# Matmuls on a constant tile in the front of a linear-attention kernel, and a new order of its loads and steps

## The chip, the cores and the metric

One Trainium2 chip, of which the program uses one core. A core has five engines that run side by side: TensorE (PE, with its weight loads as PEld), VectorE (DVE), ScalarE (ACT), GpSimd (POOL) and SyncE (SP), and 16 DMA engines that all queues share. The metric is the device time of one execution in microseconds. The kernel before took a median of 246.48 us in three runs (246.47 to 247.59).

## What is computed

Linear attention with an elu feature map over 8 batches, 8 heads, 576 positions and 64 channels, and then a multiplicative feed-forward layer on its 4608 x 512 output:

```python
def phi(x):
    return np.where(x > 0, x, np.exp(x) - 1.0) + 1.0
q_p, k_p = (phi(q), phi(k))
kv = np.einsum('bhsd,bhse->bhde', k_p, v)
z = np.sum(k_p, axis=2)
num = np.einsum('bhsd,bhde->bhse', q_p, kv)
den = np.einsum('bhsd,bhd->bhs', q_p, z)[..., None] + 1e-06
x = num / den                      # then heads side by side: 4608 x 512
a = x @ w1                         # 512 x 1024
b = x @ w2                         # 512 x 1024
h = a * b @ w3                     # 1024 x 1024
out = h @ w_out                    # 1024 x 512
```

Inputs and output are float32; the products run in bfloat16.

## The kernel before

**The work.** w3 and w_out are first multiplied into one matrix wf of 1024 x 512, so that each token goes through w1 and w2, a product of the two, and wf. The 8 batches are 8 chunks of 512 tokens; what is left of each batch (64 tokens) makes a ninth chunk. The core works through attention of batch b, then the feed-forward units of its chunk, with several chunks under way at a time.

**The order is written out by hand.** `ORDER` (from L585) is a string of steps. `step` (L638) issues each in turn, so the string gives the order on every engine and on every queue; each engine runs its own instructions strictly in that order. A step is a letter, a number, often a second number after a dot, and sometimes a `+`, which chooses another engine or queue. The letters that the text uses:

- `E i`: load row tile i of w3 (`load_w3`, L135), on POOL's queue. `w i`: eight transposes of it on PE and a copy (`w3_tr`, L145). `C x`: load a quarter of w_out (`load_wo`, L130), on POOL's queue. `u i.p`: two of the eight matmuls of row tile i of wf (`wf_mm`, L152); the copy out of PSUM comes behind the last pair.
- `L`, `M`, `N` with b.g: load half g of k, q or v of batch b (`load_qkv`, L99). With `+`, and for v of the first two batches always, the load goes on POOL's queue, else on SP's. `R b.0` is the tail of q and k as four DMAs of 64 KB, `R b.1` the tail of v as two (`load_tail`, L110); with `+` on POOL's queue. The text calls them tail pieces.
- `B x.p`: load the quarter x of the columns of w1 (p = 0) or w2 (p = 1), on POOL's queue (`load_w12`, L124).
- `X`/`x`, `Y`/`y`, `Z`/`z` with b.g: exponential (ACT), max (DVE) and min (DVE) of phi, for q (capital) and k; g = 2 is the tail, for both. `v b.g`: a copy of v, with g = 2 the tail.
- `a b.g`: transposes of phi(q) on PE and a copy. `T b.0`: the same by DMA, for later batches. `K b`: kv of a batch (`kv_full`, L228) on PE and two copies. `A b.j`: numerator and denominator of a block (`nat`, L289) on PE (tile nd) and the division on DVE; j = 4 is the tail. `P b.j`: transposes of the result on PE (tile xtp) and a copy. `D`: the same by DMA.
- `F c.f`: a unit of the feed-forward layer, four matmuls with w1 and four with w2 of 512 columns (`f_unit`, L380), then a copy on ACT and a product on DVE. F c.f reads the column quarter x = f/2, rounded down, of w1 and w2: F0.7 and F0.6 read B3, F0.5 and F0.4 B2, F0.3 and F0.2 B1. `h0` to `h3` are units 0 and 1 of chunk 0, four matmuls a step, and read B0; `i` closes them.
- `G`, `m`, `d`, `e`: the units of chunks 3 to 8 in a form with fewer products, and what prepares them. `O c.m`: eight matmuls with wf; `S`, `H`, `Q`: stores of the output. `I`: constants.

**Constants.** `I1` writes vrs[0], a tile of 128 x 520, with zeros and ones (four memsets; L88 and L90). `v0.2` later writes the tail of batch 0's v into parts of it.

**Buffers.** PSUM holds four banks that wf, F and some nd tiles share (`mm_ps`), one pair (`at_ps`) for kv and nd, and two banks, "o" and "u", for transposes and O units. Each tile waits until its bank's earlier reader is through.

**Two gates.** `GATES` makes SP's load M2.1 wait until B0.0 has landed, and R6.0 until the transposes T3.0. A gated load holds back what is behind it on SP.

**Order of the loads before.** On POOL: E4 E3 C0 E1 E0 C1 C2 C3 E5 E6 L0.1 E2 E7 M0.1 L0.0 N0.1 N0.0 M1.1 M1.0 R1.0 B3.0 L1.0 B3.1 N1.1 L1.1 R1.1 N1.0 B2.0 B2.1 B1.0 B0.0 B1.1 B0.1 R2.0 R3.0. On SP, at the same time: M0.0 R0.1 R0.0, and from M2.1 on the loads of the later batches.

Of the kernel before, what the change touches and what calls it, by code (L numbers as in the profile page):

```python
# [20 lines left out]
def kernel(  # L21
# [56 lines left out]
    def constants(part, alt):  # L78
# [6 lines left out]
        else:  # L85
# [3 lines left out]
            for g in range(2):  # L89
                eng.memset(vrs[part - 1][g * R:(g + 1) * R, :, g, :, D:E1], 1.0)  # L90
# [505 lines left out]
    y3.2 z3.2 N3.1 v2.1 F1.2 O0.1+ N3.0 S0.0 e0.2 K2 F1.5 A2.2 Z3.1 x3.0 F1.4 A2.1+ F1.1 x3.1 A2.0+
    y3.0 O0.3 T3.0 S0.1 y3.1 A2.3+ D2.0 z3.0 z3.1 v3.2 v3.0 v3.1 O1.2+ O1.3 R4.1 e1.3 R6.0+ M4.0
    M4.1 e0.0 e0.1 e0.3 K3 O1.0 A3.1+ O1.1 L4.0 A3.2+ e1.2 F2.1 A3.0+ N4.1 F2.5 A3.3+ D3.0 Y4.0 L4.1
    v4.2 F2.7 S1.1 N4.0 Y4.1 y4.2 X4.1 Z4.1 F2.2 A2.4+ x4.2 X4.0 F2.0 v4.1 z4.2 Z4.0 T4.0 F2.3 M5.1
    d3.2 L5.0 M5.0 S1.0 y6.2 L5.1 d3.0 R5.0+ F2.4 y5.2 d3.1 x6.2 x4.0 y4.0 z4.0 G3.1.1 F2.6 A3.4+  # L600
    v4.0+ y4.1 G3.1.3 x4.1 z4.1 G3.1.2 x5.2 O2.2 G3.1.4 z5.2 d3.3 G3.1.5 m3.1.5 G3.0.4 G3.0.1 K4
    z6.2 G3.0.3 G3.1.6 G3.1.7 A4.2+ G3.0.5 N5.0 y5.0 R5.1+ v5.2 m3.0.5 G3.0.2 Y5.1 X5.1 O2.3 S2.1
    G3.0.7 x5.0 Z5.1 G3.0.6 z5.0 Y5.0 A4.0+ X5.0 Z5.0 O2.1 m3.0.6 x5.1 O2.0 y5.1 L6.0 N5.1 L6.1
    G3.3.1 G3.3.4 S2.0 T5.0 A4.1+ z5.1 G3.2.1 m3.1.6 G3.3.3 G3.2.4 G3.2.3 G3.3.5 G3.3.2 v5.0 G3.2.5
    A4.3+ D4.0 G3.3.7 G3.2.2 v5.1 G3.3.6 G3.2.7 G3.2.6 m3.2.5 m3.2.6 x6.1 O3.1 x6.0 K5 m3.3.5 M6.1
    D1.1 m3.3.6 O3.3 y6.0 z6.0 y6.1 A5.2 z6.1 O3.2 d4.0 d4.1 d4.2 A5.0+ d4.3 G4.1.1 G4.1.4 R6.1 X6.1
    Y6.1 Z6.1 D3.1 O3.0 A5.1+ G4.1.3 G4.1.6 G4.0.1 G4.1.5 v6.2 G4.0.4 A5.3 G4.0.3 G4.1.7 G4.0.2
    G4.0.5 N6.0 v6.0 m4.1.5 G4.1.2 G4.3.1 G4.0.6 G4.0.7 A4.4+ G4.3.3 N7.1 G4.3.4 M6.0 Y6.0 G4.2.1
    G4.3.5 D5.0 d5.0 G4.3.6 X6.0 Z6.0 N6.1 G4.2.3 G4.2.2 G4.2.4 S3.1 G4.3.7 G4.2.5 v6.1 G5.0.4 d5.1
    m4.1.6 G4.2.6 G5.1.1 G4.2.7 m4.3.6 d5.2 K6 m4.3.5 L7.0 m4.0.5 G5.0.1 m4.2.5 G5.1.2 L7.1 d5.3  # L610
    G5.1.3 m4.0.6 G5.0.3 G5.0.6 G5.1.4 G5.0.5 G5.0.2 G5.1.5 G5.0.7 m4.2.6 G4.3.2 T6.0 A6.3+ G5.1.7
    y7.1 S3.0 x7.0 x7.1 O4.2 A6.0 R7.0 O4.1 y7.0 G5.2.1 z7.0 A6.2 z7.1 G5.1.6 G5.3.1 N7.0 G5.3.4
    G5.2.3 A6.1 G5.3.3 G5.2.2 G5.2.4 G5.3.5 x7.2 G5.2.5 G5.3.2 M7.1 G5.3.7 X7.1 M7.0 G5.2.6 m5.0.6
    G5.2.7 Y7.0 m5.2.5 R7.1 v7.2 m5.1.6 m5.1.5 m5.3.5 D6.0 d6.2 d6.0 Y7.1 A5.4+ O4.3 S4.1 d6.1
    m5.2.6 v7.1 O4.0 y7.2 z7.2 Z7.1 X7.0 Z7.0 G6.1.1 v7.0 G6.1.4 G5.3.6 O5.0 G6.1.3 G6.3.4 T7.0 S4.0
    m5.0.5 G6.1.6 d6.3 G6.0.1 D5.1 G6.1.2 A6.4+ m5.3.6 G6.1.5 G6.0.3 G6.0.4 G6.2.4 G6.0.5 K7+ G6.1.7
    G6.0.7 m6.1.6 G6.0.2 A7.1 G6.3.1 O5.2 G6.3.3 G6.0.6 G6.2.1 G6.3.5 G6.3.2 A7.4 G6.2.3 G6.3.7
    m6.0.6 G6.2.2 G6.2.6 G6.2.5 m6.2.5 O5.1 D7.1 m6.1.5 d8.0 G6.3.6 G6.2.7 d8.1 m6.3.6 S5.0 A7.3+
    O5.3 G8.0.1 G8.0.4 G8.1.1 d8.2 A7.0 G8.0.3 G8.0.6 G8.1.3 d8.3 G8.0.5 G8.1.4 G8.1.5 S5.1 G8.2.4
    G8.0.7 G8.0.2 G8.1.7 G8.1.2 m6.2.6 G8.2.1 G8.1.6 m6.0.5 G8.3.1 m6.3.5 G8.2.3 G8.2.6 G8.3.3  # L620
    m8.1.5 G8.2.5 G8.3.4 G8.3.5 G8.3.2 G8.2.7 A7.2+ G8.2.2 G8.3.7 D7.0 d7.0 m8.0.6 O6.2 O6.1 O6.0
    S6.0 O6.3 G7.0.1 d7.1 d7.3 d7.2 G8.3.6 m8.3.6 G7.1.1 S6.1 G7.0.3 G7.0.4 m8.3.5 G7.1.3 G7.0.5
    m7.0.5 G7.1.4 G7.1.5 G7.0.6 G7.0.7 G7.0.2 G7.1.7 G7.1.6 G7.2.1 G7.1.2 m8.0.5 G7.3.1 m8.1.6
    G7.2.3 G7.2.4 G7.3.3 m8.2.6 G7.3.4 G7.2.5 G7.2.2 G7.3.2 G7.3.5 G7.2.7 G7.3.6 G7.2.6 G7.3.7 O7.0
# [7 lines left out]
    def loaded(s, ins):  # L632
        s = s.rstrip("+")
        if s in gates:
            after(ins, held[gates[s]])
        held[s] = ins

    def step(s):  # L638
        alt = len(s) - len(s.rstrip("+"))
# [4 lines left out]
        if t == "F":
            f_unit(b, i)
        elif t == "G":
            g_unit(b, i, int(at[1]))
        elif t == "m":
            g_mul(b, i, int(at[1]), alt)
        elif t == "e":  # L650
            ws_make(b, i, alt)
        elif t == "d":
            xs_make(b, i, alt)
        elif t == "O":
            o_unit(b, i, alt)
        elif t == "V":
            w_unit(b, i)
        elif t == "s":
            s_make(b, i, alt)
        elif t == "S":  # L660
            o_store(b, i)
        elif t == "H":
            o_store(b, i // 2, i % 2)
        elif t == "Q":
            o_last(b, i)
        elif t == "I":
            constants(b, alt)
        elif t == "w":
            w3_tr(b, alt)
        elif t == "u":  # L670
            wf_mm(b, i, alt)
        elif t == "t":
            wt_make(b)
        elif t in "LMN":
            name = "kqv"["LMN".index(t)]
            loaded(s, load_qkv(name, b, i, alt))
        elif t == "R":
            loaded(s, load_tail(b, i, alt))
        elif t == "B":
            loaded(s, load_w12(b, i))  # L680
        elif t == "C":
            loaded(s, load_wo(b))
        elif t == "E":
            loaded(s, load_w3(b))
        elif t in "xX":
            phi_exp("kq"["xX".index(t)], b, i)
        elif t in "yY":
            phi_max1("kq"["yY".index(t)], b, i, alt)
        elif t in "zZ":
            phi_min("kq"["zZ".index(t)], b, i)  # L690
        elif t == "v":
            v_unit(b, i, alt)
        elif t == "T":
            held[s] = qt_load(b, i)
        elif t == "a":
            q_tr(b, i, alt)
        elif t == "K":
            kv_full(b, alt)
        elif t == "A":
            nat(b, i, alt)  # L700
        elif t == "D":
            xt_load(b, i)
        elif t == "P":
            xt_tr(b, i, alt)
        elif t == "h":
            if b == 0:
                held["h"] = [f_open(0, 0), f_open(0, 1)]
            for f in range(2):
                for ps, w in zip(held["h"][f], (w1_sb, w2_sb)):
                    f_mm(0, f, ps, w, b)  # L710
        elif t == "i":
            f_close(0, b, *held["h"][b])

    nc.scalar.preload_act_table_set("natural_log_exp_and_others")
    for s in ORDER.split():
        step(s)
# [28 lines left out]
```

## Time and profile before

| what | value |
|---|---|
| median of three runs | 246.48 us |
| the profiled execution | 246.08 us |
| its span, first to last instruction | 244.3 us |
| PE busy | 227.1 us (93%), 1675 matmuls |
| DVE busy | 190.0 us (78%) |
| ACT busy | 159.1 us (65%) |
| POOL busy | 37.5 us (15%) |
| mean granted TensorE clock | 0.992 |
| DMA moved | 49.46 MB, 202 GB/s in the mean |

Times inside the trace count from the first instruction, so a step at 47 us is 47 us into the span. In a row of a timeline stand the start, the duration from first start to last end, the engine, the line, the operation, the tiles it writes and reads, the shape, and the count; in brackets the idle time of the engine ahead of it, and what ended that. Matmuls overlap in the pipeline, so a price per matmul is taken from start to start, not from durations. A row of waits has who waited at which line, for whom, the total in us, how often, and the longest. A row of busy time by stretch has the stretch, its length, then busy time and count of PE, PEld, DVE, ACT and POOL, the granted clock, the DMA share (the sum over packets under way, so it can be over 1) and GB/s.

### The profile page before, as it was taken

The page shows a single profiled execution, that of the slowest core. Times are in us where ns is not written, and L with a number is a line of the kernel's source. Part 1 is how long each engine was busy: PE and PEld are TensorE (multiplying, and loading weights), DVE is VectorE, ACT ScalarE, POOL GpSimd, SP SyncE. Part 2 cuts the span into 40 slices and gives each one's busy share as a digit, 9 for nine tenths or more (in the row PEclk, how much of TensorE's full clock was granted, in tenths as well). Part 3 has the DMA queues.
Part 4 walks back from the last instruction along what each step waited for, and adds up shares of the span by engine and source line. Part 5 has one row for each costly group of instructions (what it writes and reads, how often), then busy time and mean ns, then how long its engine had stood idle before and what let it go on. Part 6 is the DMA issues. An engine that isn't in the chain of part 4 may idle for free.

```text
span 244.3 us, 4627 instructions
## 1 busy us (share of the span) xinstructions
PE 227.1 (93%) x1675; PEld 146.8 (60%) x1692; DVE 190.0 (78%) x416; ACT 159.1 (65%) x296; POOL 37.5 (15%) x61
## 2 busy tenths in 40 slices
...
GB/s 159 192 201 301 296 234 240 196 241 309 287 197 290 263 196 275 214 289 270 370 366 192 243 244 292 237 248 157 86 198 10 107 90 0 89 172 0 3 196 149
DMA packets 68343, 49.46 MB, mean 202 GB/s; under 512 B 37088, under 2 KB 63456, under 8 KB 68320
## 3 DMA queue, kind: packets, MB, share of 16 engines
...
## 4 chain that ended last, share of the span: by engine, by line
PE 67%; DMA 15%; DVE 7%; ACT 6%; issue 2%; POOL 1%; SPq 0%; DVEq 0%; ACTq 0%; POOLq 0%
PE o_ps L544 21%; PE gu L429 14%; PE gt L429 10%; PE a_ps L366 7%; PE b_ps L366 7%; DMA k<-in_k_dram 5%; DMA q<-in_q_dram 5%; PE nd L311 3%; DMA wt_sb<-in_moe_w_out_dram 3%; DMA v<-in_v_dram 3%; ACT e L181 2%; PE kvp L246 1%; DVE spare L464 1%; ACT spare L461 1%; DVE y L186 1%
## 5 line engine op out<-in xcount | busy, mean ns | idle before, releaser
L544 PE MATMUL o_ps<-wf_sb,ab 128*128 128x512 bf16 x266 | 63.1, 379 | 0.8
L544 PEld LDWEIGHTS <-ab 128*128 128x128 bf16 x280 | 26.9, 98 | 29.1 <-DVE ab L468 0.8
L546 ACT COPY o_sb<-o_ps 128x512 f32<-128x512 f32 x31 | 18.1, 585 | 26.1 <-PE o_ps L544 24.9
L429 PEld LDWEIGHTS <-w_sb 128*128 128x128 bf16 x288 | 27.9, 98 | 5.7 <-issue 0.9
L366 PEld LDWEIGHTS <-w_sb 128*128 128x128 bf16 x192 | 18.4, 100 | 20.2 <-issue 1.7
L366 PE MATMUL a_ps<-xt,w_sb 128*128 128x512 bf16 x96 | 26.5, 389 | 0.0
L366 PE MATMUL b_ps<-xt,w_sb 128*128 128x512 bf16 x96 | 26.1, 384 | 0.0
L330 DVE TENSOR_TENSOR xn<-nd,r 128x512 bf16<-128x512 f32 x30 | 20.7, 691 | 2.1
L372 DVE TENSOR_TENSOR ab<-a_sb,b_ps 128x512 bf16<-128x512 f32 x24 | 16.2, 684 | 6.5 <-PE b_ps L366 3.3
L429 PEld LDWEIGHTS <-wt_sb 128*128 128x128 bf16 x192 | 18.2, 98 | 4.0 <-issue 0.2
L429 PEld LDWEIGHTS <-spare 128*128 128x128 bf16 x192 | 18.7, 98 | 2.2
L181 ACT ACTIVATE e<-q 128x1024 bf16<-128x1024 f32 x16 | 16.9, 1059 | 3.7 <-DMA q<-in_q_dram 3.7
L473 DVE TENSOR_TENSOR ab<-spare 128x256 bf16<-128x256 f32 x48 | 18.5, 418 | 0.1
L429 PE MATMUL gu<-spare,wt_sb 128*128 128x256 bf16 x96 | 18.3, 272 | 0.1
L429 PE MATMUL gu<-spare 128*128 128x256 bf16 x96 | 18.3, 272 | 0.0
L311 PE MATMUL nd<-kv,qt 128*128 128x130 bf16 (+1 forms) x160 | 15.9, 221 | 2.5 <-DVE r L317 1.2
L371 ACT COPY a_sb<-a_ps 128x512 f32<-128x512 f32 x24 | 13.7, 584 | 6.5 <-PE a_ps L366 6.4
L464 DVE TENSOR_TENSOR spare<-spare,gu 128x512 f32<-128x512 f32 x24 | 16.2, 680 | 2.0 <-PE gu L429 1.9
L464 DVE TENSOR_TENSOR spare<-spare,gt 128x512 f32<-128x512 f32 x24 | 16.2, 680 | 1.9 <-PE gt L429 1.9
L181 ACT ACTIVATE e<-k 128x1024 bf16<-128x1024 f32 x16 | 16.9, 1060 | 0.4 <-DMA k<-in_k_dram 0.3
L156 PE MATMUL wf_ps<-wt_sb,w3t 128*128 128x512 bf16 x61 | 16.2, 408 | 0.9 <-DMA wt_sb<-in_moe_w_out_dram 0.7
L311 PEld LDWEIGHTS <-qt 128*128 128x128 bf16 (+1 forms) x160 | 11.0, 99 | 9.7 <-DVE xn L330 4.7
...
## 6 DMA issues: line engine op xcount, KB each, us to landing
...
```

Source lines behind the costliest of these rows:

```text
L156: nc.tensor.matmul(wfs[i], w3ts[i][:, kc, :], wo_sb[:, kc, :], start=(kc == 0), stop=(kc == FC - 1))
L181: nc.scalar.activation(out=e, in_=x, func=AF.Exp)
L311: nc.tensor.matmul(nds[g][rows, i * 2 * E1:(i + 1) * 2 * E1], w, kvs[b % 2][:, i, g].rearrange("p u e -> p (u e)"), start=True, stop=True)
L330: nc.vector.tensor_tensor(out=dst.rearrange("p (g h) e -> p g h e", g=2), in0=v4[:, :, :, 0:D], in1=r[rows].unsqueeze(3).to_broadcast([n, ...
L366: nc.tensor.matmul(ps, w[:, kc, f * P:(f + 1) * P], xt_of(c)[:, :, kc, :], start=(kc == 0), stop=(kc == KC - 1))
L371: nc.scalar.copy(out=a_sb, in_=a_ps)
L372: nc.vector.tensor_mul(out=abs_[c][:, f, :], in0=a_sb, in1=b_ps)
L429: nc.tensor.matmul(t[:, w], l, r, start=(first and w == 0 and k == 0), stop=(k == 1), skip_group_check=True)
L464: nc.vector.tensor_tensor(out=s, in0=s, in1=t, op=ALU.add)
L473: (nc.gpsimd if alt else nc.vector).tensor_mul(out=abs_[c][:, f, r * HN:(r + 1) * HN], in0=s[:, 0], in1=s[:, 1])
L544: nc.tensor.matmul(o_ps, ab[:, f, m * P:(m + 1) * P], wf_sb[:, f, :], start=(f == 0), stop=(f == FC - 1))
L546: copy_of(alt)(out=rows_of(c, m // 2)[:, m % 2], in_=o_ps)
```

## The change

A function `spin(n)` issues n matmuls of 512 columns on the constant tile vrs[0] into a bank of the shared four; nothing reads the result. The step `W k.n` calls it. Four such steps are put into `ORDER`, with 8, 5, 4 and 3 matmuls: W0.8 ahead of w4, W1.5 between w4 and w3, W2.4 between w3 and w1, W3.3 between u1.0 and u3.0.

The order from the ninth load on is new. On POOL: E4 E3 C0 E1 E0 C1 C2 as before, then C3 E7 M0.1 R0.0 N0.0 L0.0 L0.1 E5 N0.1 R1.1 E6 E2 B3.0 M1.1 M1.0 R1.0 B3.1 L1.0 L1.1 N1.0 N1.1 R3.0 B2.0 B2.1 R3.1 B0.1 B0.0 R2.0 B1.0 B1.1. On SP: M0.0 R0.1, then M2.1, still behind its gate on B0.0, R2.1, L2.0 and so on. R0.0 and R3.1 have gone from SP's queue to POOL's. On PE, w5, w6 and w2 and their products come later, among the steps of batch 0's attention. F0.7 is followed by a1.1, F0.6, K1, a1.2, A1.3, F0.4, A1.0, F0.5; then come h0 to h3, and F0.2 and F0.3 behind them.

The rest of `ORDER` has the same steps in another order, to the end. The two sections of it that the text speaks of, with the code:

```diff
+    def spin(n):
+        ps = mm_ps.tile([P, NCH], F32, tag="mm", name="spin")
+        z = vrs[0].rearrange("p i g u e -> p (i g u e)")
+        for _ in range(n):
+            nc.tensor.matmul(ps, z[:, 0:P], z[:, 0:NCH], start=True, stop=True)
...
     ORDER = """
-    E4 E3 C0 E1 E0 I0 M0.0 C1 I1+ C2 I2+ w4 w3+ R0.1 v0.2 Y0.0 u4.0 u3.0 C3 w1+ R0.0 E5 w0+ E6 L0.1+
-    E2 u1.0 u0.0 E7 M0.1+ u4.1 u3.1 L0.0+ u0.1 x0.2 u0.2 u3.2 y0.2 u1.1 u1.2 z0.2 u3.3+ u4.2 u4.3
-    u1.3 w5+ w6 N0.1 N0.0+ u0.3+ u5.0 u5.1 u6.0 u6.1 X0.0 y0.1 Z0.0 M1.1+ u6.2 x0.1 u6.3+ z0.1 w2
-    Y0.1 X0.1 w7 M1.0+ R1.0+ B3.0 L1.0+ Z0.1 u5.2 y0.0 u5.3 u2.0 u2.1 x0.0 u2.2 u2.3+ B3.1 a0.0+
-    z0.0 u7.0 u7.1 a0.1+ X1.1 Y1.1 u7.2 K0 N1.1 L1.1+ X1.0 I3 Z1.1 a0.2 R1.1+ Y1.0 u7.3 A0.2 a1.1
-    A0.3 A0.0 P0.2 A0.1 Z1.0 x1.2 x1.0 y1.0 P0.3 A0.4 y1.2 N1.0 P0.0 P0.1 y1.1 B2.0 v1.2 z1.2 x1.1
-    B2.1 a1.0 z1.0 B1.0 z1.1 F0.7 F0.6 K1+ F0.4 a1.2 A1.2 F0.5 B0.0 I4 P1.2 A1.1 B1.1 F0.2 B0.1 P1.1
-    M2.1 M3.1 A1.3 F0.3 P1.3 X2.1 R2.0+ A1.0 L2.1 h0 h1 Y2.1 P1.0 M2.0 h2 h3 Z2.1 i0 i1 X3.1 R3.0+
-    A1.4 x2.1 F1.7 F1.6 x2.2 y2.2 Y2.0 M3.0 z2.2 e1.0 R2.1 x3.2 X2.0 Z2.0 N2.0 y2.1 z2.1 L2.0 O0.0
...
+    E4 E3 C0 E1 E0 I0 M0.0 C1 I1+ C2 I2+ W0.8 w4 W1.5 w3+ R0.1 C3 E7 M0.1+ X0.0 Y0.0 Z0.0 R0.0+
+    N0.0+ L0.0+ L0.1+ Y0.1 y0.2 E5 v0.2 N0.1 R1.1+ E6 E2 B3.0 W2.4 M1.1+ M1.0+ R1.0+ B3.1 L1.0+ w1
+    L1.1+ N1.0 w0 u0.0 u0.1 u0.2 u4.0 u0.3+ w7 N1.1 R3.0+ B2.0 B2.1 R3.1+ u4.1 u4.2 a0.0 x0.2 z0.2
+    u4.3+ B0.1 X0.1 Z0.1 B0.0 u7.0 u7.1 u7.2 u7.3+ x0.0 y0.0 R2.0+ z0.0 u1.0 W3.3 u3.0 a0.2+ B1.0
+    y0.1 a0.1+ x0.1 z0.1 u3.1 u3.2 u1.1 u3.3+ v1.2+ M2.1 u1.2 u1.3+ R2.1 w5 K0 I3 B1.1 w6 A0.3 L2.0
+    A0.0+ A0.1 w2 u6.0 P0.3+ u6.1 u6.2 A0.2 u5.0 X1.1 Y1.0 u5.1 P0.0+ u6.3 N2.0 Y1.1 X1.0 Z1.0 Z1.1
+    u5.2 u5.3 A0.4+ L2.1 P0.2 u2.0 y1.2 P0.1 x1.2 z1.2 M2.0 x1.0 y1.0 z1.0 y1.1 x1.1 z1.1 u2.1 u2.2
+    u2.3 a1.0+ F0.7 a1.1+ F0.6 K1+ I4 a1.2+ A1.3+ F0.4 A1.0+ F0.5 P1.3+ A1.2+ h0 h1 N2.1 N3.1 L3.0
+    M3.0 P1.0 e0.0 A1.1 y3.2 h2 h3 i0 i1 y2.2 A1.4+ P1.2 P1.1+ Y2.1 L3.1 e1.0 F0.2 F0.3 e0.2 F1.1
+    e1.2 X2.1 Z2.1 x2.1 F1.2 x3.2 z3.2 F1.5 X2.0 Y2.0 Z2.0 x2.2 z2.2 T2.0 v2.2 x2.0 O0.1+ y2.0 z2.0
...
     GATES = "R6.0<T3.0 M2.1<B0.0"
...
-        elif t == "V":
-            w_unit(b, i)
+        elif t == "W":
+            spin(i)
```

More of the change, by code (lines that the diff above doesn't have):

```diff
@@ L596 @@
[L596 to L624, printed above, removed]
@@ new lines @@
+    x6.2 x4.1 F2.5 L4.0 F2.0 D3.0 d3.0 d3.1 d3.2 x4.0 N4.1 F2.4 F2.3 X5.0 d3.3 G3.1.1 y4.1 z4.1 L5.0
+    v4.1 N4.0 T4.0 G3.1.4 y4.0 z4.0 O2.2 M5.1 G3.1.2 G3.1.3 A2.4 G3.0.1 G3.0.4 S1.1 G3.1.5 v4.0
+    m3.1.5 G3.1.6 G3.0.3 G3.0.6 G3.1.7 R5.0+ y5.2 y6.2 K4+ L5.1 x5.0 G3.0.5 N5.1 y5.0 x5.2 Z5.0
+    m3.0.6 O2.3 A4.2+ G3.0.7 Y5.1 G3.0.2 X5.1 Z5.1 O2.1 z5.2 A4.1+ x5.1 R5.1+ y5.1 z5.1 O2.0 G3.3.1
+    G3.3.4 m3.0.5 A4.0+ G3.2.1 z5.0 G3.3.3 G3.3.2 G3.2.4 G3.2.3 G3.3.5 G3.2.2 G3.2.5 N5.0 v5.0
+    G3.2.6 L6.1 G3.3.7 S2.1 A4.3+ G3.2.7 v5.1 m3.1.6 v5.2 G3.3.6 O3.1 K5 m3.2.6 m3.2.5 m3.3.6 x6.1
```

28 lines of the change are left out of this document (25 added, 3 removed).

## The prediction

> **What bounds the kernel now.** I read the head of the page first, then the busy time by stretch, the chain of waits, the timelines of TensorE (PE) and of the POOL queue, and last the waits of the weight loads.
>
> ```profile
> span 244.3 us, 4627 instructions
> core 0: us, PE busy (x) PEld busy (x) DVE busy (x) ACT busy (x) POOL busy (x), PEclk, DMA share, GB/s
> 35.80:39.20 3.40, 1.70 (x20) 1.19 (x18) 3.26 (x12) 3.40 (x7) 3.40 (x5) 1.00 1.35 258
> 39.20:42.70 3.50, 3.43 (x15) 1.75 (x15) 2.92 (x8) 1.05 (x4) 1.61 (x3) 0.51 1.39 220
> 42.70:60.00 17.30, 17.30 (x136) 9.45 (x135) 12.62 (x28) 11.12 (x18) 5.74 (x10) 1.00 1.20 243
> 60.00:90.00 30.00, 29.84 (x177) 15.01 (x179) 26.40 (x51) 20.94 (x37) 3.43 (x6) 1.00 1.11 254
> 90.00:180.00 90.00, 88.53 (x678) 60.78 (x683) 83.63 (x185) 74.37 (x146) 2.68 (x5) 1.00 0.95 243
> 180.00:230.00 50.00, 49.79 (x400) 37.81 (x403) 38.34 (x88) 29.38 (x64) 0.00 (x0) 1.00 0.27 75
> ```
>
> From 42.7 to 230 us PE is busy 185.46 of 187.30 us: there is next to nothing to win behind the front. Ahead of that, for 3.4 us from 39.2, the granted clock is half (0.51 over 3.5 us), behind a stretch with 1.70 busy of 3.40. So at first sight PE sets the end from about 39 us on, and warming it would pay. But the DMA share is over 1 from 35.8 to 90 us, and the chain of waits runs over loads until 33 us:
>
> ```profile
> 10.37 11.36 DMA k<-in_k_dram
> 21.73 0.28 issue
> 22.02 11.31 DMA q<-in_q_dram
> ```
>
> A load issued at 10.37 lands 11.36 us later, and 0.28 us after that landing POOL issues the next: it keeps eight loads in flight and starts an issue 0.28 us after the load eight issues earlier has landed. So the POOL timeline shows landings. These issues wait (idle time in brackets), in order, for E3, C3, N0.1, N1.0, B2.0, B2.1, B0.0 and B0.1:
>
> ```profile
> 8.62 0.55 POOL L139 DMA_DIRECT2D w3b<-in_moe_w_dram  x1 [1.07 <-DMA w3b<-in_moe_w_dram]
> ...
> 18.05 0.75 POOL L101 DMA_DIRECT2D vt<-in_v_dram  x1 [0.68 <-DMA wt_sb<-in_moe_w_out_dram]
> ...
> 28.99 0.76 POOL L127 DMA_DIRECT2D w_sb<-in_moe_w_dram  x1 [0.64 <-DMA vt<-in_v_dram]
> ...
> 44.78 0.63 POOL L116 DMA_DIRECT2D qk32r<-in_q_dram  x1 [0.68 <-DMA vt<-in_v_dram]
> 46.08 0.62 POOL L116 DMA_DIRECT2D qk32r<-in_k_dram  x1 [0.67 <-DMA w_sb<-in_moe_w_dram]
> 47.42 0.62 POOL L116 DMA_DIRECT2D qk32r<-in_k_dram  x1 [0.72 <-DMA w_sb<-in_moe_w_dram]
> ...
> 50.18 0.62 POOL L116 DMA_DIRECT2D qk32r<-in_q_dram  x1 [0.42 <-DMA w_sb<-in_moe_w_dram]
> ...
> 52.79 0.62 POOL L116 DMA_DIRECT2D qk32r<-in_k_dram  x1 [0.74 <-DMA w_sb<-in_moe_w_dram]
> ```
>
> Less 0.28 each: E3 at 8.34, C3 17.77, N0.1 28.71, N1.0 44.50, B2.0 45.80, **B2.1 47.14**, **B0.0 49.90**, B0.1 52.51. Now PE around them:
>
> ```profile
> 40.07 1.91 PE L366 MATMUL a_ps<-xt,w_sb 128*128 128x512 bf16 x4
> 41.78 1.46 PE L366 MATMUL b_ps<-xt,w_sb 128*128 128x512 bf16 x4
> ...
> 47.20 1.03 PE L366 MATMUL b_ps<-xt,w_sb 128*128 128x512 bf16 x4
> 48.07 0.28 PE L278 MATMUL tpr<-ident,qj 128*128 128x128 bf16 x2
> 48.18 0.39 PE L311 MATMUL nd<-kv,qt 128*128 128x130 bf16 x4
> 48.41 1.03 PE L366 MATMUL a_ps<-xt,w_sb 128*128 128x512 bf16 x4
> ...
> 54.94 0.38 PE L366 MATMUL a_ps<-xt,w_sb 128*128 128x512 bf16 x1
> ...
> 56.66 0.39 PE L345 MATMUL xtp<-ident,xn 128*128 128x128 bf16 x4
> 56.88 0.38 PE L366 MATMUL a_ps<-xt,w_sb 128*128 128x512 bf16 x1
> ```
>
> F0.4's second half reads B2.1 and starts at 47.20, 0.06 us after it has landed; the waits of the weight loads between 46.5 and 48.9 us say the same:
>
> ```profile
> PEld L366 <- DMA w_sb<-in_moe_w_dram: 0.3, 1, 0.3
> ```
>
> The front is thus bound twice: PE, and the loads right beside it. **A faster PE wins nothing unless B2.1 lands earlier.**
>
> **The change part by part.** Prices from starts in the rows above: a 512-column matmul takes (41.78-40.07)/4 = 0.43 us at half clock and (48.07-47.20)/4 = 0.22 at full; four nd 0.23 (48.18 to 48.41), four xtp 0.22 (56.66 to 56.88), a half of h0 and h1 1.72 (54.94 to 56.66), an F unit 1.73.
>
> 1. *Four runs, 8+5+4+3 matmuls.* They add 20 matmuls, 4.3 us at full clock, 8.6 at half.
>
> ```profile
> 5.86 1.03 PE L149 MATMUL w3p<-ident,w3b 128*128 128x128 bf16 x8 [5.86 <-DMA w3b<-in_moe_w_dram]
> 8.38 1.04 PE L149 MATMUL w3p<-ident,w3b 128*128 128x128 bf16 x8 [1.49 <-DMA w3b<-in_moe_w_dram]
> 1.98 0.18 DVE L90 MEMSET vr<- 64x4 bf16 x2
> ```
>
> The tile is set at 2.16, so the run of 8 fits ahead of 5.86 (3.4 us). The run of 5 (2.1 us) overruns the 1.49 us gap by 0.6; the run of 4 waits for v0.2 and may hold w1 by up to 1 us; the run of 3 is 0.65 us. I cost them at nothing: PE's wait ahead of F0.4 hides them (below). With that cover gone they cost up to 2.3 us. A clock that is up by 15 us, and no half clock at 39 us, would give PE 1 to 1.7 us, which it then waits.
>
> 2. *R0.0 goes from SP's queue to POOL's.* Four tail pieces. On POOL the four of R1.0 landed from 33.33 (M1.0, in the chain) to 27.33+7.7 = 35.0, 1.65 us for four:
>
> ```profile
> 27.33 1.02 POOL L116 DMA_DIRECT2D qk32r<-in_k_dram  x1 [0.80 <-DMA k<-in_k_dram]
> qk32r<-in_k_dram POOLq DMA_DIRECT2D x1, 64.0 KB, 7.7
> 18.47 0.63 ACT L181 ACTIVATE er<-qk32r 128x512 bf16<-128x512 f32 x1 [7.42 <-DMA qk32r<-in_k_dram]
> ```
>
> On SP they were under way until 18.4 (er waits for them). From E3 (8.34) to C3 (17.77) six POOL loads took 1.57 us each; the next eight, to N0.1 (28.71), 1.37 each. The 0.2 x 6 = 1.2 us is what SP's pieces cost the POOL loads, so the move costs 1.65-1.2 = 0.45 us. Bounds: 0 (mere exchange) and 1.0 (if other pieces caused most of the slow stretch). I take **0.5**.
> The Trainium skill ("DMA: Bandwidth & Descriptors", Issuing engines are not separate DMA queues) says that DMAs from any engine run on the same 16 DMA engines and interleave; by it the move costs nothing and the sum below would be 0.5 us less.
>
> 3. *The order of POOL's loads.* Up to B2.1 the list holds the same loads as before, in another order (E7, M0.1, N0.0, L0.0, L0.1 ahead of E5, E6, E2), and one more: R3.0, four pieces, now ahead of B2.0. Then R3.1 (two pieces) precedes B0.1 and B0.0, and R2.0 (four) B1.0 and B1.1. Four pieces are 1.65 by the row, two 0.8; bounds 0 (if they slip in beside the other loads) and 1.65. I take **1.5**, near the row. So B2.1 lands at 47.14+0.5+1.5 = **49.1**, B0.0 at 49.90+0.5+1.5+0.8 = **52.7**, the last of B1 at 52.51+0.5+1.5+0.8+1.5 = 56.8.
>
> 4. *PE's order.*
>
> ```profile
> 30.06 0.23 PE L240 MATMUL kvp<-vt,kj 128*128 128x128 bf16 x1
> ...
> 32.87 0.39 PE L311 MATMUL nd<-kv,qt 128*128 128x130 bf16 x4 [0.56 <-ACT kv L255]
> 33.09 0.61 PE L284 MATMUL tp<-ident,qj 128*128 128x128 bf16 x8
> 33.54 0.39 PE L311 MATMUL nd<-kv,qt 128*128 128x130 bf16 x4
> ```
>
> K0 and the copies of kv take 2.8 us (30.06 to 32.87), eight transposes 0.45 (33.09 to 33.54). An estimate from these rows: C3 lands about 1 us sooner without R0.0 on SP, and the seven loads E7 to N0.1 with R0.0's pieces bring N0.1 to 16.8+7x1.37+1.65 = 28.0. K0 and the copies of kv end at 30.9 (z0.1 hardly later than N0.1); then two late w3 tiles' transposes (0.9), the products of three (24 matmuls, 5.2), five nd (1.15), four xtp (0.9) and a1.0 (0.45) make 8.6 and put F0.7 at 39.5, at full clock. F0.7, a1.1, F0.6 end at 43.4. K1 wants N1.1: the same loads stand ahead of it as ahead of N1.0 before (44.50), so 45.0; then K1 and the copies of kv, 2.8, half a microsecond of it done ahead of N1.1 (they now stall PE: A1.3 stands in F0.4's old place), A1.3 0.23 and F0.4's first half 0.87: PE would want B2.1 at 48.4. It gets it at 49.1; the loads decide, by 0.7 us. Every wait on DVE and ACT that the new order moves lies in that cover; without the cover each counts fully.
>
> 5. *From there.* F0.4's second half 0.87, A1.0 0.23, F0.5 1.73, P1.3 and A1.2 0.45: 52.4; h0 waits for B0.0, 52.7. h0 to h3 3.46, P1.0, A1.1, A1.4, P1.2, P1.1 1.12: F0.2 at 57.3, its second half at 58.2, after B1 (56.8). In the kernel before, the same work is left at h0 (54.94), where F0.2 and F0.3 are done instead, except P1.0 and A1.4, 0.45. From 54.94 to the end are 189.36 us; so the end is at 57.3+189.36-0.45 = 246.2, **+1.9 us**.
>
> 6. *The order behind.* Re-ordered throughout, with the same instructions. M2.1 is gated on B0.0 as before, now 2.8 us later, and x2.1 on ACT stands ahead of F1.2's copy. PE's idle time from 60 to 230 us is 1.84 us, which bounds a gain; a loss I bound by the same. I take 0.
>
> Sum against the profiled execution: 246.08 around a span of 244.3; 246.2+1.78 = **248.0 us**. The runs shown have a median 0.4 above that execution (246.48), so 248.0 lies 0.6% over the median.
>
> **The rivals.**
> *A, the half clock comes back.* From 43.4 to 49.1 PE has 2.75 us of matmuls in 5.7, no denser than the 1.70 in 3.40 that preceded the half clock. 3.4 us at half cost 1.7, less the 0.3 that h0 waits: 249.4. Against: where the stretch falls is open.
> *B, the pieces are hidden.* If tail pieces cost the loads nothing, PE's own path decides with N1.1 at 44.5: F0.4's second half at 47.9, F0.2 at 55.8 against the 54.94+0.45 = 55.4 of no change: 246.5. For: a share over 1 says that packets overlap. Against: the 1.65 us of R1.0.
> *C, faster: PE's clock and the filled waits decide.* If B2.1 is no later than PE wants it and K1 isn't held, and the copies of kv come under other work, F0.4's second half starts at 43.4+1.5 (K1 alone)+0.3 (A1.3, a1.2)+0.9 = 46.1, F0.2 at 54.0, 1.4 before no change: 244.7. It decides once B2.1 lands a microsecond earlier than before, with more ahead of it. The half clock at 39.2 speaks for it, the 0.06 us behind B2.1 against.
> The Trainium skill ("TensorE: Matmul & The Clock Gate", Why this matters for your kernels) advises against idle gaps over some 3 us and for 4 us of steady matmuls; the rows at 35.8 to 42.7 agree, and no row shows that these runs are enough.
>
> **How the numbers follow.** Forecast 0.50, A 0.15, B 0.18, C 0.17. The forecast's own range is 247.4 (no cost of the move, 1.4 for R3.0) to 249.3 (1.0 and 1.65, and 0.7 from step 6). To hold 8 in 10 the range goes from 245.4, which takes in B and a little of C, to 250.0, which takes in A. About 0.5% can be told from no change: faster is under 245.25, slower over 247.71. Slower: A and 0.42 of the forecast, 0.57. Within: the forecast's rest but 0.02 and nearly all of B, 0.24. Faster: C and that rest, 0.19.
>
> **What would show it.** Right: POOL's waits put B2.1 at 48.5 to 49.7; F0.4's second half starts right behind it; PE has idle time ahead of it that was not there; the half clock at 39 us is gone and the clock is up before 15 us. Step 2 is wrong if C3 lands later than 17; step 3 if four R3.0 pieces take under 1 us; step 5 if h0 starts before B0.0 is due at 52; step 6 if PE's idle time from 60 to 230 us changes by over 1 us. The prediction falls if B2.1 lands before 47.5, or if the loss lies behind 60 us.

## The result, and the profile after

| | before | after |
|---|---|---|
| median of the runs compared (lowest to highest) | 247.03 us (246.47 to 247.72) | 253.72 us (251.40 to 254.65) |
| ratio, with its 95% interval | | 1.0251 (1.0203 to 1.0298) |
| the profiled execution, its span | 246.08, 244.3 us | 254.65, 252.6 us |
| mean granted clock | 0.992 | 0.980 |

The changed kernel is 2.5% slower. The head of its page, and then the busy time in the stretches that the prediction used (columns as in the prediction):

```profile
span 252.6 us, 4689 instructions
...
PEclk9959999999799999999999999999999999999999
```

```profile
35.80:39.20 3.40, 3.40 (x29) 1.83 (x27) 3.30 (x7) 3.40 (x7) 3.40 (x5) 1.00 1.10 304
39.20:42.70 3.50, 3.40 (x27) 1.82 (x25) 2.90 (x6) 2.36 (x4) 2.68 (x4) 1.00 1.27 210
42.70:60.00 17.30, 15.95 (x127) 8.81 (x127) 14.24 (x31) 6.97 (x15) 6.97 (x11) 1.00 1.15 215
60.00:90.00 30.00, 26.54 (x139) 12.39 (x138) 23.35 (x44) 20.17 (x31) 0.00 (x0) 0.94 0.86 238
90.00:180.00 90.00, 86.73 (x664) 58.38 (x663) 80.91 (x179) 68.44 (x132) 6.25 (x10) 1.00 1.01 243
180.00:230.00 50.00, 50.00 (x407) 37.89 (x406) 42.42 (x95) 30.75 (x66) 0.00 (x0) 1.00 0.35 92
```

Two things are to be seen. The half clock at 39 us is gone, and PE is busy for 6.80 of the 6.90 us from 35.8 to 42.7. But from 60 to 230 us, where PE stood 1.84 us before, it now stands 3.46 + 3.27 + 0 = 6.73 us, and the clock has two dips elsewhere, at 11.9 and at 66.5. The loss lies behind 60 us. PE's timeline shows the places (start, duration, engine, line, operation, tiles, shape, count, and in brackets the idle time ahead and what ended it):

```profile
6.27 1.24 PE L97 MATMUL spin<-vr 128*128 128x512 bf16 x5
...
11.06 1.06 PE L97 MATMUL spin<-vr 128*128 128x512 bf16 x4 [2.31 <-ACT vr L228]
...
39.40 1.03 PE L372 MATMUL a_ps<-xt,w_sb 128*128 128x512 bf16 x4
...
46.63 0.40 PE L317 MATMUL nd<-kv,qt 128*128 128x130 bf16 x4 [0.86 <-DVE kv L261]
...
47.74 0.82 PE L372 MATMUL b_ps<-xt,w_sb 128*128 128x512 bf16 x3
...
51.27 0.39 PE L372 MATMUL a_ps<-xt,w_sb 128*128 128x512 bf16 x1
...
56.08 1.03 PE L372 MATMUL a_ps<-xt,w_sb 128*128 128x512 bf16 x4
...
65.75 1.14 PE L372 MATMUL b_ps<-xt,w_sb 128*128 128x512 bf16 x4 [3.46 <-ACT a_sb L377]
66.68 1.91 PE L372 MATMUL a_ps<-xt,w_sb 128*128 128x512 bf16 x4
68.39 1.80 PE L372 MATMUL b_ps<-xt,w_sb 128*128 128x512 bf16 x4
70.02 1.24 PE L550 MATMUL o_ps<-wf_sb,ab 128*128 128x512 bf16 x5
...
97.62 0.59 PE L372 MATMUL a_ps<-xt,w_sb 128*128 128x512 bf16 x2 [1.08 <-DMA xt<-xn]
...
110.42 0.81 PE L372 MATMUL a_ps<-xt,w_sb 128*128 128x512 bf16 x3 [1.24 <-ACT a_sb L377]
```

The front runs as forecast in its shape: F0.7 at 39.40, F0.4's second half at 47.74, h0 at 51.27, F0.2 at 56.08, which is 0.7 us behind the 55.4 of no change. Then come one wait of 3.46 us ahead of F1.2's second half; eight matmuls at half clock behind it, 3.34 us from 66.68 to 70.02 where eight at 0.216 take 1.73, so 1.6 lost; a wait for the transposes D2.0, and one more behind ACT at 110 us. Idle time 6.73 - 1.84 = 4.9, half clock 1.6 and front 0.7 make 7.2 of the 8.3 us between the two spans; the rest I do not assign (the execution before has 17 fewer matmul records than weight loads, so its idle time is over-stated).

What ended the wait of 3.46 us is in ACT's timeline, and where that came from is in the chain of waits:

```profile
61.21 1.06 ACT L187 ACTIVATE e<-q 128x1024 bf16<-128x1024 f32 x1
64.17 1.06 ACT L187 ACTIVATE e<-k 128x1024 bf16<-128x1024 f32 x1 [1.90 <-DMA k<-in_k_dram]
65.13 0.57 ACT L377 COPY a_sb<-a_ps 128x512 f32<-128x512 f32 x1
```

```profile
51.24 0.41 SPq L112
...
54.28 9.87 DMA k<-in_k_dram
...
64.17 0.02 ACT e L187
```

B0.0 lands at 51.23 and opens the gate; M2.1 goes out at 51.24 (the chain's SP row), but L2.1, the k half that x2.1 reads, stands behind M2.1, R2.1, L2.0 and N2.0 on SP: it goes out at 54.28 and lands at 64.15. ACT runs in order; x2.1 stands ahead of the copy of F1.2's first half, and F1.2's second half waits for that copy (I take it that the copy frees its bank; the trace names the copy, not the bank). A late load on one queue thus holds an instruction on a second engine and stops a third.

### The profile page after: what moved, and what is told of

Same layout as the page of the kernel before. It is cut to its first block, busy times and chain, and to the rows that moved or that the text cites. A ratio compares the mean times of both kernels' runs of the same rounds, so it can differ in the third digit from the quotient of the medians.

```text
span 252.6 us, 4689 instructions
## 1 busy us (share of the span) xinstructions
PE 233.4 (92%) x1712; PEld 148.7 (59%) x1712; DVE 194.9 (77%) x427; ACT 155.9 (62%) x285; POOL 42.5 (17%) x67
## 4 chain that ended last, share of the span: by engine, by line
PE 56%; DMA 27%; SPq 4%; DVE 3%; POOL 3%; issue 3%; ACT 2%; ACTq 0%; DVEq 0%; POOLq 0%
PE o_ps L550 23%; PE gu L435 12%; DMA k<-in_k_dram 10%; PE gt L435 9%; DMA w3b<-in_moe_w_dram 4%; DMA q<-in_q_dram 4%; PE b_ps L372 3%; PE a_ps L372 3%; DMA vt<-in_v_dram 3%; SPq L122 2%; DMA w_sb<-in_moe_w_dram 2%; PE kvp L252 2%; PE nd L317 2%; DMA qk32r<-in_k_dram 2%; DMA v<-in_v_dram 2%
## 5 line engine op out<-in xcount | busy, mean ns | idle before, releaser
L550 PE MATMUL o_ps<-wf_sb,ab 128*128 128x512 bf16 x280 | 64.2, 379 | 0.0
L552 ACT COPY o_sb<-o_ps 128x512 f32<-128x512 f32 x28 | 16.3, 585 | 28.1 <-PE o_ps L550 26.3
L435 PEld LDWEIGHTS <-spare 128*128 128x128 bf16 x192 | 18.7, 98 | 2.2
L479 DVE TENSOR_TENSOR ab<-spare 128x256 bf16<-128x256 f32 x48 | 19.1, 419 | 0.3
L192 DVE TENSOR_SCALAR y<-q 128x1024 bf16<-128x1024 f32 x16 | 11.0, 687 | 9.9 <-DMA q<-in_q_dram 9.9
L162 PE MATMUL wf_ps<-wt_sb,w3t 128*128 128x512 bf16 x64 | 17.5, 413 | 1.2 <-ACT w3t L156 1.2
```

Source lines behind the costliest of these rows:

```text
L162: nc.tensor.matmul(wfs[i], w3ts[i][:, kc, :], wo_sb[:, kc, :], start=(kc == 0), stop=(kc == FC - 1))
L435: nc.tensor.matmul(t[:, w], l, r, start=(first and w == 0 and k == 0), stop=(k == 1), skip_group_check=True)
L479: (nc.gpsimd if alt else nc.vector).tensor_mul(out=abs_[c][:, f, r * HN:(r + 1) * HN], in0=s[:, 0], in1=s[:, 1])
L550: nc.tensor.matmul(o_ps, ab[:, f, m * P:(m + 1) * P], wf_sb[:, f, :], start=(f == 0), stop=(f == FC - 1))
L552: copy_of(alt)(out=rows_of(c, m // 2)[:, m % 2], in_=o_ps)
```

## The experiments

Each ratio below is to the kernel before, measured beside it, with its 95% interval; the changed kernel has 1.0251 (1.0203 to 1.0298). The edits show the words of `ORDER` around the place, not whole lines.

### What the spins cost

**e1.** The changed kernel without its four W steps.

```diff
- C2 I2+ W0.8 w4 W1.5 w3+
+ C2 I2+ w4 w3+
- B3.0 W2.4 M1.1+
+ B3.0 M1.1+
- u1.0 W3.3 u3.0
+ u1.0 u3.0
```

> The changed kernel without its four runs on the constant tile. Theory A (the loss is batch 2's k half L2.1, which lands at 64.15 us while ACT's exponential x2.1 waits for it ahead of F1.2's copy, so that PE stands 3.5 us and then runs 3.4 us at half clock): the stall stays, 253 to 255 us. Rival B (the 20 matmuls themselves cost the time, 4.3 us at full clock and 8.6 at half): 245 to 250 us.

Median 252.40 us (250.41 to 253.84), ratio 1.0218 (1.0145 to 1.0291). The interval holds the changed kernel's ratio: the spins do not cause the loss, and if they cost or save anything it is less than these four runs can tell. The wait is there without them, and behind it four matmuls take 1.86 us, so the half clock is there too (timeline of PE):

```profile
65.35 1.86 PE L372 MATMUL b_ps<-xt,w_sb 128*128 128x512 bf16 x4 [2.27 <-ACT a_sb L377]
```

**e12.** The other side of it: the kernel before with W0.8 and W1.5 and nothing else.

```diff
- C2 I2+ w4 w3+
+ C2 I2+ W0.8 w4 W1.5 w3+
```

> The kernel before with two of the four runs of spins alone, W0.8 ahead of w4 and W1.5 ahead of w3, and no change of order. If the spins cost nothing and bring the full clock of the front forward from 15.3 us: 0.3 to 1.5 us faster, ratio 0.994 to 0.999, if PE's front is bound by its clock there; if it is bound by its loads (first B1, B0 landing as before), the same time within 0.3 us.

Median 247.83 us (246.56 to 249.41, 12 runs), ratio 1.0029 (1.0004 to 1.0055): no gain, rather a loss of 0.6 to 0.7 us. In the profiled execution the half clock at 39 us starts at 36 now and lasts twice as long (busy time by stretch):

```profile
36.00:42.70 6.70, 6.03 (x41) 4.00 (x40) 6.46 (x19) 5.00 (x10) 5.33 (x8) 0.52 1.30 230
```

That this is what ate the warmer start is not shown: it is one execution of twelve. The kernel before bears on it without any edit. Of its 62 executions beside the experiments, 17 had a mean granted clock of 0.999 or 1.0, so no such half clock, and their median is 247.73 us, against 247.12 for the other 45; in the largest of the four comparisons they are 0.9 us longer than the others, in the three smaller ones 0.2 to 0.9 shorter. No gain from a full clock can be read from them, so the half clock at 39 us, which the spins were to remove, may have cost nothing.

### The wait of 3.46 us

**e2.** x2.1 goes behind F1.5 on ACT; loads and all else as in the changed kernel.

```diff
- e1.2 X2.1 Z2.1 x2.1 F1.2 x3.2 z3.2 F1.5 X2.0
+ e1.2 X2.1 Z2.1 F1.2 x3.2 z3.2 F1.5 x2.1 X2.0
```

> The changed kernel with one step moved: x2.1 stands behind F1.5 and not ahead of F1.2. Theory A: F1.2's copy no longer waits for L2.1, the 3.46 us of PE's idle time and the half clock behind it go, 5 us less: 248 to 250 us. Rival B or C (the front as a whole is late): no more than 1 us less, 252.5 to 254.

Median 250.50 us (250.03 to 250.95), ratio 1.0146 (1.0112 to 1.0181). One step moved on ACT takes back 1% of the 2.5%, a little less than expected. The same place in its timeline of PE:

```profile
62.63 1.02 PE L372 MATMUL b_ps<-xt,w_sb 128*128 128x512 bf16 x4 [0.67 <-ACT a_sb L377]
...
93.36 0.81 PE L372 MATMUL a_ps<-xt,w_sb 128*128 128x512 bf16 x3 [1.63 <-DMA xt<-xn]
```

**e3.** x2.1 stays, and L2.1 goes second on SP, right behind M2.1.

```diff
- v1.2+ M2.1 u1.2
+ v1.2+ M2.1 L2.1 u1.2
- A0.4+ L2.1 P0.2
+ A0.4+ P0.2
```

> The changed kernel with one load moved on SP's queue: L2.1 directly behind M2.1, ahead of R2.1, L2.0 and N2.0. Theory A: L2.1 lands at about 61 us and not at 64.15, PE's stall shrinks to under 0.7 us and no half clock follows, 248 to 250 us. Rival C (loads behind 51 us are late as a whole, whichever comes first): the stall goes to another step and the time stays above 252.

Median 251.65 us (250.79 to 253.06), ratio 1.0199 (1.0152 to 1.0245). That is more than the 248 to 250 us expected, and the stall did not fall under 0.7 us: in its ACT timeline no wait for the load is left, but both exponentials still stand ahead of the copy, and PE waits 1.45 us:

```profile
61.20 1.06 ACT L187 ACTIVATE e<-q 128x1024 bf16<-128x1024 f32 x1
62.17 1.04 ACT L187 ACTIVATE e<-k 128x1024 bf16<-128x1024 f32 x1
63.11 0.57 ACT L377 COPY a_sb<-a_ps 128x512 f32<-128x512 f32 x1
```

Together the three kernels take the 3.46 us apart: 2.0 for the load (3.46 to 1.45), 0.8 for x2.1's own time on ACT (1.45 to 0.67), and 0.67 that stays in e2. That rest is the copy itself, not X2.1 ahead of it. In e2's ACT timeline X2.1 is through at 61.93, and the copy starts at 61.99, as soon as PE is through with F1.2's first half (60.93 + 1.03 = 61.96 in its timeline of PE), and ends at 62.58, 0.05 us before PE goes on:

```profile
60.87 1.06 ACT L187 ACTIVATE e<-q 128x1024 bf16<-128x1024 f32 x1
61.99 0.59 ACT L377 COPY a_sb<-a_ps 128x512 f32<-128x512 f32 x1
```

The load's lateness is the largest part, but the place on ACT costs even with the load on time.

### Which half of the new order costs

**e4.** The new order with its spins up to i1, without SP's loads of batches 2 and 3; from there the old order, those loads included.

```diff
- v1.2+ M2.1 u1.2 u1.3+ R2.1 w5
+ v1.2+ u1.2 u1.3+ w5
...
- h2 h3 i0 i1 y2.2 A1.4+ P1.2 P1.1+ Y2.1 L3.1
+ h2 h3 i0 i1 P1.2 F0.2 P1.1 M2.1 M3.1 F0.3
```

> The new order and the four runs up to the closing of chunk 0's units 0 and 1, but SP's loads of batches 2 and 3 and all that follows in the old order. Theory A (front costs about 0.4 us at most, the rest lies behind 56 us): 246.5 to 248.5 us, within 0.5% of the kernel before. Rival C (the front's loads are what is late): 250 us or more.

Median 247.31 us (246.15 to 249.56, 10 runs), ratio 1.0023 (0.9982 to 1.0064): **what the new front is worth, in either direction, these runs cannot tell from nothing**; the interval goes from 0.4 us faster to 1.6 us slower.

**e5.** The old order up to i1, then the steps that are left in the new order, which takes in SP's loads behind the first four (M2.1 M3.1 L2.1 M2.0); no spins.

```diff
- h2 h3 Z2.1 i0 i1 X3.1 R3.0+ A1.4 x2.1 F1.7 F1.6
+ h2 h3 Z2.1 i0 i1 R3.0+ R3.1+ R2.1 L2.0 N2.0 N2.1 N3.1 L3.0 M3.0 e0.0 y3.2 y2.2 A1.4+ L3.1
+ e1.0 e0.2 F1.1 e1.2 x2.1 F1.2
```

> The old order, without the four runs, up to the closing of chunk 0's units 0 and 1 (with the old order of the loads of batch 2), and the new order behind. If the new order of the compute steps costs time by itself (D2.0 and F2 late, ACT behind k loads at 105 us): 249 to 251 us. If only the order of batch 2's loads does: 247 to 248 us.

Median 250.08 us (249.32 to 252.61, 10 runs), ratio 1.0128 (1.0089 to 1.0166). The new order behind i1, steps and loads together, costs 1.3% with the old front, too. Its timeline of PE has the waits:

```profile
74.35 0.40 PE L252 MATMUL kvp<-vt,kj 128*128 128x130 bf16 x4 [0.66 <-DVE kj L216]
...
93.37 1.02 PE L372 MATMUL a_ps<-xt,w_sb 128*128 128x512 bf16 x4 [1.35 <-DMA xt<-xn]
...
103.50 1.02 PE L372 MATMUL a_ps<-xt,w_sb 128*128 128x512 bf16 x4 [0.44 <-ACT a_sb L377]
...
106.00 1.02 PE L372 MATMUL a_ps<-xt,w_sb 128*128 128x512 bf16 x4 [0.61 <-ACT a_sb L377]
...
157.00 0.40 PE L317 MATMUL nd<-kv,qt 128*128 128x130 bf16 x4 [0.59 <-DMA qt<-qj]
```

They sum to 3.65 us. The kernel before has 0.43 and 0.45 behind 60 us, so 2.8 us more, against 3.2 between the spans of the two executions (247.5 and 244.3) and 2.8 between the medians of that comparison (250.08 and 247.25). These are small waits in five places: at each, the step that PE needs is ready 0.4 to 1.4 us after PE gets there. The wait of 3.46 us is not among them: with the old front and L2.1 third on SP, F1.2 runs without one. So the 2.5% come apart: about 1.3 for the order behind i1 by itself (e5), 0.2, not told from nothing, for the front (e4), and the 1.0 that e2 takes back, which needs both L2.1 late on SP and x2.1 ahead of F1.2.

**e11.** One of the five: e2 with A2.1 and its transposes D2.0 ahead of F1.6.

```diff
- A2.0 e0.1 v3.0 F1.6 S0.1 A2.1+ D2.0
+ A2.0 e0.1 v3.0 A2.1+ D2.0 F1.6 S0.1
```

> The kernel of e2 (x2.1 behind F1.5) with A2.1 and D2.0 ahead of F1.6, where PE reaches A2.1 8 matmuls (1.73 us) earlier. In e2, xt of batch 2 was issued by SP at 85.48 and landed 93.32, and PE stood 1.63 us for it. SP is held by T3.0 until 84.80, so D2.0 is issued some 0.7 us earlier. If the lateness of D2.0 in the new order is what is left there: the wait ahead of the first F2 falls from 1.63 us to 0.8 to 1.0 and the time by about 0.7 us to 249.5 to 250, ratio 1.010 to 1.013. If the transfers beside it set its landing (its last 4.5 us passed after the issue): it lands at 93.3 again, the wait is as long as F1.6's shift lets it be, and the time is that of e2 within 0.3 us.

Median 249.68 us (249.17 to 251.46), ratio 1.0125 (1.0073 to 1.0176). The wait for xt is gone altogether, more than I expected, and nearly as much came back earlier, because A2.1 now waits for A2.0's division (timeline of PE):

```profile
82.22 0.40 PE L317 MATMUL nd<-kv,qt 128*128 128x130 bf16 x4 [1.24 <-DVE xn L336]
```

1.63 us saved, 1.24 paid: the span is 247.6 against 248.0 for e2. F1.6 had stood between the two for a reason.

### Loads and steps apart

**e6.** e4 with SP's loads of batches 2 and 3 as early as in the changed kernel and in its order (but M3.1 ahead of L3.1); the steps that read them stay in the old order.

```diff
- v1.2+ u1.2 u1.3+ w5
+ v1.2+ M2.1 u1.2 u1.3+ R2.1 w5
...
- P1.1 M2.1 M3.1 F0.3 X2.1 L2.1 Y2.1 M2.0 Z2.1 X3.1
+ P1.1 M3.1 F0.3 X2.1 Y2.1 Z2.1 X3.1
```

> As e4, new up to the closing of units 0 and 1 and old behind, but SP's loads of batches 2 and 3 in the new order too. Theory A (SP's order brings L2.1 fifth, at 64 us, and x2.1 waits for it): a stall of PE of 2 us or more between 58 and 66 us, 249.5 to 252 us. Rival (the load order is harmless, only the compute order behind costs): 247 to 248 us, as e4.

Median 259.44 us (258.21 to 260.52), ratio 1.0443 (1.0367 to 1.0518), the slowest of all, far over the 249.5 to 252 us expected, and not for the reason expected (x2.1). X3.1 reads M3.1, which this list has behind ten others; ACT stands 11.63 us for it, and PE behind ACT 9.24 (timelines of ACT and of PE):

```profile
72.33 1.06 ACT L187 ACTIVATE e<-q 128x1024 bf16<-128x1024 f32 x1 [11.63 <-DMA q<-in_q_dram]
```

```profile
74.85 1.86 PE L372 MATMUL a_ps<-xt,w_sb 128*128 128x512 bf16 x4 [9.24 <-ACT a_sb L377]
```

**e7.** The changed kernel with the first twelve of those loads nearly in the old order (M2.1 M3.1 L2.1 M2.0 M3.0 R2.1 N2.0 L2.0 N2.1 N3.1 L3.0 L3.1).

```diff
- v1.2+ M2.1 u1.2 u1.3+ R2.1 w5
+ v1.2+ M2.1 u1.2 u1.3+ M3.1 w5
- w6 A0.3 L2.0
+ w6 A0.3 L2.1
```

> The changed kernel with the first twelve loads on SP behind the gate in nearly the old order (M2.1 M3.1 L2.1 M2.0 M3.0 R2.1 N2.0 L2.0 N2.1 N3.1 L3.0 L3.1). Theory A: L2.1 lands at about 62.5, the stall at 62 us shrinks to about 1.5 us, as in e3; what stays is the compute order behind: 250 to 252 us. Rival (the load order is the whole loss): 247 to 248.5 us.

Median 252.24 us (251.37 to 253.12), ratio 1.0154 (1.0084 to 1.0225). L2.1 is third there, and the wait ahead of F1.2's second half is 1.45 us as in e3. So the new steps cost 1.5% with nearly the old loads, near the 1.3% of e5, and the old steps cost 4.4% under the new loads: an order of steps can be judged only with the loads that it runs beside. By the median of all 13 runs of the kernel before in that comparison, 247.25 us, the ratios of e6, e7 and e8 would be 1.049, 1.020 and 1.027, so the 1.5% may be 2.0.

### Could the front gain?

Forecast step 3 says that the tail pieces ahead of B2 cost the front. **e8** is e4 with R2.0, R3.1 and R3.0 behind B1.1 on POOL, and with A1.3, A1.0 and A1.2 behind F0.4, F0.5 and h1.

```diff
- N1.1 R3.0+ B2.0 B2.1 R3.1+ u4.1
+ N1.1 B2.0 B2.1 u4.1
- y0.0 R2.0+ z0.0
+ y0.0 z0.0
- I3 B1.1 w6
+ I3 B1.1 R2.0+ R3.1+ R3.0+ w6
- a1.2+ A1.3+ F0.4 A1.0+ F0.5 P1.3+ A1.2+ h0 h1 P1.0
+ a1.2+ F0.4 A1.3+ F0.5 A1.0+ P1.3+ h0 h1 A1.2+ P1.0
```

> As e4, with the tail pieces R3.0, R3.1 and R2.0 behind B1.1 on POOL's queue again, and F0.4 ahead of A1.3, F0.5 ahead of A1.0. If B2.1 and B0.0 set the front: B2.1 lands at about 46.7 us, PE no longer stands for the copies of kv, and the time is 1 to 1.5 us below e4, 245.5 to 246.5 us. If something else sets it: as e4, 247 to 248.

Median 253.89 us (252.14 to 255.01), ratio 1.0214 (1.0132 to 1.0297). The front gained what was looked for, h0 at 48.96 against 51.27, and lost it twice over: y3.2, left where the new front has it, held DVE for the tail of k that now came last, and the products of chunk 0 queued behind it (timelines of PE and of DVE):

```profile
48.96 0.38 PE L372 MATMUL a_ps<-xt,w_sb 128*128 128x512 bf16 x1
...
61.06 1.87 PE L372 MATMUL a_ps<-xt,w_sb 128*128 128x512 bf16 x4 [4.29 <-DVE ab L378]
```

```profile
59.99 0.43 DVE L192 TENSOR_SCALAR yr<-qk32r 128x512 bf16<-128x512 f32 x1 [5.94 <-DMA qk32r<-in_k_dram]
```

**e9** puts y3.2 back to its old place as well, and **e10** is e9 without the four W steps.

```diff
- P1.0 e0.0 A1.1 y3.2 h2 h3
+ P1.0 e0.0 A1.1 h2 h3
- e1.1 z3.2
+ e1.1 y3.2 z3.2
```

> The new front with the three r tails behind B1.1 on POOL, as in e8, but with y3.2 at its old place behind Y3.1, so that DVE no longer waits for R3.0 (landed 59.80 in e8) ahead of the products of F0; loads and order of batches 2 and on as before. If that wait alone made e8's stall of 4.29 us and the half clock behind it: no stall near 56 us, h0 as in e8 (48.96 against 51.27 in the changed kernel), granted clock full from 56 to 66, and a time of 243.5 to 246 us, ratio 0.985 to 0.997. If the front's 2.3 us are given back by the loads of batches 2 and on, which come no earlier than before: a stall for q, k or v between 56 and 75 us and a ratio of 1.00.

> The kernel of e9 without the four W steps; it computes the same. If the spins are worth what the half clock of the front costs: half clock until 15 us or later and 1 to 2.5 us more than e9, ratio to the kernel before 0.99 to 1.005. If PE's waits for loads in the front decide (W3.3 and W2.4 stand in waits of 1 to 2.3 us), the two kernels agree within 0.5 us.

e9: median 247.27 us (246.32 to 248.75, 12 runs), ratio 1.0002 (0.9971 to 1.0033). e10: 247.23 (245.62 to 248.91, 12 runs), 0.9993 (0.9958 to 1.0028). The stall and the half clock behind it went, as expected; the gain that I expected did not come. The timeline of PE in e9:

```profile
49.28 0.38 PE L372 MATMUL a_ps<-xt,w_sb 128*128 128x512 bf16 x1
...
52.79 0.40 PE L317 MATMUL nd<-kv,qt 128*128 128x130 bf16 x4 [1.17 <-DVE xn L336]
...
54.98 1.03 PE L372 MATMUL a_ps<-xt,w_sb 128*128 128x512 bf16 x4
```

h0 is 2.0 us earlier than in the changed kernel, but A1.1 waits 1.17 us for A1.2's division, which my edit put right ahead of it, and F0.2 starts at 54.98, 0.4 before the 55.4 of no change. Neither of the two ways that I had expected: the rest was given back ahead of F0.2, not at the loads of batch 2. And the spins, all four, are worth nothing here that twelve runs can tell: the medians of e9 and e10 differ by 0.04 us.

No version beats the kernel before.

## Why the prediction was wrong

The direction was right (slower), the time was not: 248.0 us with a range to 250.0, and 253.72 measured. The direction was luck in the main: the 1.9 us that made the forecast slower were to come from the front, where 0.7 was found, and the loss came from the step that I had put at nothing. By the prediction's own sign, a loss behind 60 us, it fell. By its steps:

1. *Four runs at no cost.* Right: e1 and e10. That they would bring an earlier clock which PE then waits out held too. In this execution a half clock came back all the same. The run of 4 waited for v0.2, as feared ("may hold w1 by up to 1 us"): 2.31 us of idle time stand ahead of it, and the clock was half from 11.9 to 18.7. In e2, e3, e4 and e9, with the same four runs, the granted clock is 1.00 from 8.5 to 18.7.

2. *R0.0 to POOL, +0.5.* Wrong size, and sign. A row of POOL's timeline and two of the chain of the changed kernel:

```profile
16.64 0.76 POOL L112 DMA_DIRECT2D k<-in_k_dram  x1 [0.52 <-DMA wt_sb<-in_moe_w_out_dram]
```

```profile
36.67 7.28 DMA vt<-in_v_dram
43.94 0.28 issue
```

C3 lands at 16.64 - 0.28 = 16.36 (17.77 before). N1.1 lands at 43.94 with the same loads ahead of it as N1.0 before at 44.50, so -0.6 us where I took +0.5 and bounded by 0. The rule that I set beside it, the Trainium skill's ("DMA: Bandwidth & Descriptors", Issuing engines are not separate DMA queues: transfers of all queues share the engines), gave nothing for the move and was nearer. No run moves R0.0 alone, so how much of the -0.6 us is the move's own, and how much the new order's, stays open.

3. *The tail pieces.* Right in kind, somewhat too dear. From N1.1 to B2.1 (F0.4's second half starts at 47.74, right behind it) are 3.8 us, against 47.14 - 44.50 = 2.6 before, where the same two loads lie between without R3.0: 1.1 for the four pieces where I took 1.5. R3.1's two: B0.0 at 51.23 is 3.5 behind B2.1, 2.8 before, so 0.7 against 0.8. B2.1 came 0.6 us later than before, not 2.0, and so ahead of the 48.5 to 49.7 that was to show the forecast right.

4. *PE's order.* Right in the main: F0.7 at 39.40 (39.5), a wait for the copies of kv ahead of A1.3 (0.86 us), PE at F0.4's second half when its load lands. But the load does not decide by 0.7 us, as forecast: F0.4's first half starts at 46.87 and takes 0.87, so PE gets to the second half at 47.74 and starts it at once. The waits of the weight loads name w_sb there as before:

```profile
PEld L372 <- DMA w_sb<-in_moe_w_dram: 0.3, 1, 0.3
```

5. *From there.* h0 at 51.27, 0.04 behind B0.0: the mechanism held. F0.2 at 56.08 against 57.3; the difference comes from steps 2 and 3, which had B0.0 1.5 us too late. So the front cost 0.7 us in this execution, and e4 could not tell it from nothing; its end lies between rival B's (F0.2 at 55.8) and the forecast's.

6. *"The order behind … I take 0."* **This step failed.** It named the pair that did it, M2.1 gated on B0.0 and x2.1 ahead of F1.2's copy, and priced it by the wrong bound: PE's idle time from 60 to 230 us, 1.84 us, bounds what a new order can gain there. It says nothing of what one can lose. A loss has no such bound: each wait that the old order had hidden can come out, and e6 shows 9.24 us from one. What could have been worked out from the trace of before: there the gate opened at 49.90, and SP's loads behind it (issue plus time to landing) landed at 56.25, 57.91, 59.87 (L2.1, third), 61.90 and 63.73, the first after 6.3 us and the next every 1.9. In the new list L2.1 has, behind M2.1, the two pieces of R2.1 and two halves more ahead of it. With the forecast's own gate (52.7) and its 0.8 for two pieces that is 52.7 + 6.3 + 0.8 + 3 x 1.9 = 65.5, while PE would be through with F1.2's first half at 57.3 + 3 x 1.73 + 0.87 = 63.4: a wait of 2 us, and x2.1's own time on top. With the measured gate (51.2) and 0.7 for the pieces it is 63.9, and it came at 64.15, while PE is through with F1.2's first half at 62.1. The two later places, at 97.6 and 110.4 us in the changed kernel, would still have been missed.

Of the rivals, A (a half clock returns) came true in another place: not between 43 and 49 us but behind the wait that the order made. It is part of the loss and not needed for it: two of the four runs of the changed kernel had a mean granted clock of 0.999 and 1.0, with spans of 249.3 and 251.1 us. B was near for F0.2 (55.8), but the pieces did cost something. C did not come true: B2.1 landed later than before and the copies of K1's kv held PE for 0.86 us. Whether a front could gain what C says stays open: e9, with the pieces out of the way, has F0.2 only 0.4 us ahead, but with the wait of 1.17 us that my edit made.

What stays open: the 1.3% of the new order behind i1 were shown as a whole (e5) and tried in one place (e11); whether the others can be mended one by one, or come back elsewhere as in e11, was not tried.
